# Four slots ahead of the feed-forward, and weights in six slices: a retention layer fused with a bilinear feed-forward

## The chip, the cores and the metric

The kernel runs on one core of a Trainium2 chip. The metric is device microseconds of one execution. Before the change it is 255.87 us, the median of three runs (255.71 to 256.0). The profiled execution, from which all durations below come, has a span of 254.2 us from the first to the last instruction.

## The reference

The first half is a decayed linear attention (retention) over 4 batches, 8 heads, 768 positions and 64 channels a head:

```python
for t in range(S):
    state = gamma * state + outer(k[:, :, t], v[:, :, t])
    y[:, :, t] = scale * q[:, :, t] @ state          # gamma = 1 - 2**(-5 - head)
```

Its output is laid out as x of 3072 tokens by 512 channels and goes through a bilinear feed-forward with d_ff = 1536:

```python
out = ((x @ w_a) * (x @ w_b)) @ w_out
```

Inputs and output are float32.

## The kernel before, in words

**Slots.** A slot is 128 positions of one batch, all heads: 6 slots a batch, 24 in all. For each slot three loads fetch k, q and v (256 KB each, in rows of 256 bytes, `load_slot`, L86). `casts` makes bfloat16 copies: kb (k with its decay, on VectorE for the slots of the first tile, on GpSimd for later ones), qb (GpSimd) and vb (ScalarE for the first tile, else GpSimd). Then three steps run on TensorE. `step_a` transposes kb and qb into PSUM (L181, L183), and VectorE copies both out as kqT (L185). `step_b` forms the scores `at` of the slot from kqT (L193), which VectorE masks into aT (L197), and adds the slot to the running state `st` (L203), which ScalarE copies to gst (L210); the last slot of a batch needs no state. `step_c` forms y from the state (L218, not for the first slot of a batch) and from aT (L223), and ScalarE copies it into xt (L228), where it is the transposed input of the feed-forward.

**Tiles.** `TILES` groups consecutive slots into tiles. For tile J the feed-forward runs 12 blocks (`ffn_ab`): block ft has four matmuls into `a` (L253), which ScalarE copies to asb (L256), and four into `g` (L259), which VectorE multiplies by asb into ht (L261). A matmul is as wide as the tile: 128 columns for each slot. `a` and `g` share three PSUM buffers. Then `ffn_out` runs once for each slot of the tile: 12 matmuls of 512 columns (L266), a copy on ScalarE (L269), and the store (L271).

**Weights.** w_a and w_b are loaded in slices by columns (`load_w`, L93), w_out in four parts by rows (`load_o`, L99), each into a float32 staging tile with a number of buffers (`bufs`), and cast to bfloat16 by `cast_w` and `cast_o` (L143, L145). A slice serves `FPW` blocks: three blocks with four slices. Only tile 0 has to wait for weights; from tile 1 on they are all in place.

**The order.** Each engine runs its instructions strictly in the order of the program, which `seq` fixes. All loads go through SyncE's queue in the order of the list `LOADS`; a load into a staging buffer waits until the cast that reads the buffer's last content is done, and everything behind it in that queue waits too. `run` mixes the blocks of the feed-forward (`work`) with the attention steps of later slots (`todo`): step i is placed just before the work item with number `at[i]`, and the casts of a slot are placed up to `ahead` items before its `step_a`. In the stages of tiles 2 to 6 the steps of the next tile are spread evenly.

**The start.** The first tile's slots run with nothing beside them. Then `ab0` runs the blocks of tile 0, and after the last block of slice j it places the casts of slice j+1. On VectorE that cast (0.95 us) thus stands behind the ht of that block.

Of the kernel before, what the change touches and what calls it, by code (L numbers as in the profile page):

```python
# [9 lines left out]
F32 = mybir.dt.float32  # L10
# [2 lines left out]
ALU = mybir.AluOpType  # L13


TILES = [3, 2, 4, 4, 4, 4, 3]


LOADS = ("s0 s1 s2 w0 w1 s3 w2 s4 w3 o0 o1 o2 o3 "
         + " ".join(f"s{t}" for t in range(5, 24))).split()  # L20


@with_exitstack
def kernel(
# [10 lines left out]
    nc = tc.nc  # L35
    P = 128
# [3 lines left out]
    DM = H * D  # L40
    DFF = moe_w_a.shape[1]
    KT = DM // P
    NFT = DFF // P
    NSLOT = B * NCH
    NW = 4
    WC = DFF // NW
    FPW = NFT // NW
    MID = S // 2

    lg = [math.log(1.0 - 2.0 ** (-5.0 - h)) for h in range(H)]  # L50
# [3 lines left out]
    wstage = ctx.enter_context(tc.tile_pool(name="wstage", bufs=4))  # L54
# [24 lines left out]
    raws, wst = {}, {}  # L79
# [8 lines left out]

    def load_w(j):
        for nm, src in (("a", moe_w_a), ("b", moe_w_b)):  # L90
            st = wstage.tile([P, KT, WC], F32, tag="w" + nm, name="wst" + nm, bufs=2)
            s = src[:, j * WC : (j + 1) * WC].rearrange("(c p) f -> p c f", p=P)
            seq(nc.sync.dma_start(out=st, in_=s))  # L93
            wst[nm, j] = st

    def load_o(j):
        st = wstage.tile([P, FPW, DM], F32, tag="wo", name="wsto", bufs=2)
        s = moe_w_out[j * FPW * P : (j + 1) * FPW * P, :].rearrange("(c p) d -> p c d", p=P)
        seq(nc.sync.dma_start(out=st, in_=s))  # L99
        wst["o", j] = st  # L100

    pending = list(LOADS)

    def issue_loads(n):
        for _ in range(min(n, len(pending))):
            what = pending.pop(0)
            {"s": load_slot, "w": load_w, "o": load_o}[what[0]](int(what[1:]))
# [29 lines left out]
    wa_bf = wpool.tile([P, KT, DFF], BF16, name="wa_bf")  # L137
    wb_bf = wpool.tile([P, KT, DFF], BF16, name="wb_bf")
    wo_bf = wpool.tile([P, NFT, DM], BF16, name="wo_bf")

    def cast(engine, dst, src):
        if engine is nc.scalar:
            seq(nc.scalar.copy(dst, src))  # L143
        else:
            seq(engine.tensor_copy(dst, src))  # L145

    def cast_w(j):
        sl = slice(j * WC, (j + 1) * WC)
        cast(nc.scalar if j == 0 else nc.gpsimd, wa_bf[:, :, sl], wst["a", j])
        cast(nc.vector, wb_bf[:, :, sl], wst["b", j])  # L150

    def cast_o(j):
        cast(nc.gpsimd, wo_bf[:, j * FPW : (j + 1) * FPW, :], wst["o", j])


    kb, qb, vb, kqT, aT = {}, {}, {}, {}, {}
# [2 lines left out]
    first = 0  # L159
    for J, n in enumerate(TILES):  # L160
        for i in range(n):
# [4 lines left out]
    def casts(t):  # L166
        ci = t % NCH
        early = t < TILES[0]
        kb[t] = nat.tile([P, H, D], BF16, tag="kb", name="kb")
        qb[t] = nat.tile([P, H, D], BF16, tag="qb", name="qb")  # L170
        vb[t] = nat.tile([P, H, D], BF16, tag="vb", name="vb")
        seq((nc.vector if early else nc.gpsimd).tensor_tensor(  # L172
            kb[t], raws["k", t], ktab[:, ci, :, :].to_broadcast([P, H, D]), op=ALU.mult))
        seq(nc.gpsimd.tensor_tensor(  # L174
            qb[t], raws["q", t], qtab[:, ci, :, :].to_broadcast([P, H, D]), op=ALU.mult))
        cast(nc.scalar if early else nc.gpsimd, vb[t], raws["v", t])

    def step_a(t):
        tp = psat.tile([P, 2, HP, P], BF16, tag="at", name="tp")
        for hp in range(HP):  # L180
            seq(nc.tensor.transpose(tp[:, 0, hp, :], kb[t][:, 2 * hp : 2 * hp + 2, :], ident))  # L181
        for hp in range(HP):
            seq(nc.tensor.transpose(tp[:, 1, hp, :], qb[t][:, 2 * hp : 2 * hp + 2, :], ident))  # L183
        kqT[t] = tra.tile([P, 2, HP, P], BF16, tag="kqT", name="kqT")
        seq(nc.vector.tensor_copy(kqT[t], tp))  # L185

    def step_b(t):
        ci = t % NCH
        at = [psat.tile([P, HP, P], F32, tag="at", name=f"at{e}") for e in range(2)]
        for hp in range(HP):  # L190
            for e in range(2):
                r = slice(64 * e, 64 * e + 64)
                seq(nc.tensor.matmul(at[e][:, hp, :], kqT[t][r, 0, hp, :], kqT[t][r, 1, hp, :],  # L193
                                     start=True, stop=True))
        aT[t] = tra.tile([P, 2, HP, P], BF16, tag="aT", name="aT")
        for e in range(2):
            seq(nc.vector.tensor_tensor(aT[t][:, e], at[e], mask, op=ALU.mult))  # L197
        if ci < NCH - 1:
            if ci == 0:
                state[0] = psst.tile([P, HP, P], F32, tag="st", name="st")  # L200
            st = state[0]
            for hp in range(HP):
                seq(nc.tensor.matmul(st[:, hp, :], kb[t][:, 2 * hp : 2 * hp + 2, :],  # L203
                                     vb[t][:, 2 * hp : 2 * hp + 2, :],
                                     start=(ci == 0 and hp == 0), stop=(hp == HP - 1),
                                     skip_group_check=True))
            g = gst[(t + 1) % 2]
            for e in range(2):
                r = slice(64 * e, 64 * e + 64)
                seq(nc.scalar.copy(g[r, :, r], st[r, :, r]))  # L210

    def step_c(t):
        ci = t % NCH
        J, i = where[t]
        y = psat.tile([P, HP, P], F32, tag="at", name="y")
        if ci > 0:
            for hp in range(HP):
                seq(nc.tensor.matmul(y[:, hp, :], gst[t % 2][:, hp, :], kqT[t][:, 1, hp, :],  # L218
                                     start=(hp == 0), stop=False, skip_group_check=True))
        for hp in range(HP):  # L220
            for e in range(2):
                r = slice(64 * e, 64 * e + 64)
                seq(nc.tensor.matmul(y[r, hp, :], vb[t][:, 2 * hp + e, :], aT[t][:, e, hp, :],  # L223
                                     start=(ci == 0 and hp == 0), stop=(hp == HP - 1),
                                     skip_group_check=True))
        if i == 0:
            xt[J] = xtp.tile([P, KT, 4 * P], BF16, tag="xt", name="xt")
        seq(nc.scalar.copy(xt[J][:, :, i * P : (i + 1) * P], y))  # L228

    def steps(slots):  # L230

        slots = list(slots)
        todo = []
        for i in range(len(slots) + 1):
            if i < len(slots):
                todo.append((step_a, slots[i]))
            if i > 0:
                todo.append((step_c, slots[i - 1]))
            if i < len(slots):
                todo.append((step_b, slots[i]))  # L240
        return todo
# [4 lines left out]
    def ffn_ab(J, ft):  # L246
        w = TILES[J] * P
        if ft == 0:
# [14 lines left out]
    def ffn_out(J, i):  # L263
# [5 lines left out]
        seq(nc.scalar.copy(osb, o))  # L269
        n0 = (sum(TILES[:J]) + i) * P  # L270
        seq(nc.scalar.dma_start(out=out[n0 : n0 + P, :], in_=osb))  # L271


    def run(work, todo, at, ahead=4):

        order = []
        for g, w in enumerate(work):
            order += [todo[i] for i in range(len(todo)) if at[i] == g]
            order.append(w)
        starts = [s for fn, s in todo if fn is step_a]  # L280
        for i, (fn, *args) in enumerate(order):
            for fn2, *a2 in order[i : i + ahead + 1]:
                if fn2 is step_a and a2[0] in starts:
                    starts.remove(a2[0])
                    casts(a2[0])
            fn(*args)

    def ab0(ft):
        ffn_ab(0, ft)
        if ft % FPW == FPW - 1 and ft // FPW + 1 < NW:  # L290
            cast_w(ft // FPW + 1)

    casts(0)
    casts(1)
    step_a(0)
    casts(2)
    step_b(0)
    step_a(1)
    step_c(0)
    step_b(1)  # L300
    step_a(2)
    step_c(1)
    step_b(2)
    cast_w(0)
    step_c(2)
    issue_loads(100)

    work = [(ab0, ft) for ft in range(NFT)] + [(ffn_ab, 1, ft) for ft in range(6)]
    todo = steps([3, 4])
    run(work, todo, [6, 7, 9, 10, 11, 12], ahead=3)  # L310
    for j in range(NW):
        cast_o(j)
    work = [(ffn_ab, 1, ft) for ft in range(6, NFT)]
    work += [(ffn_out, 0, i) for i in range(TILES[0])]
    work += [(ffn_out, 1, i) for i in range(TILES[1])]
    todo = steps(range(5, 9))
    run(work, todo, [3, 4, 5, 6, 6, 7, 7, 8, 8, 9, 9, 10])
    slot = sum(TILES[:3])
    for J in range(2, len(TILES)):
        n = TILES[J]  # L320
# [2 lines left out]
        todo = steps(nxt)  # L323
        work = [(ffn_ab, J, ft) for ft in range(NFT)] + [(ffn_out, J, i) for i in range(n)]
# [31 lines left out]
```

## Time and profile before

| What | Value |
|---|---|
| median of 3 runs | 255.87 us (255.71 to 256.0) |
| profiled execution, span | 254.2 us |
| TensorE busy | 233.5 us (92%) |
| VectorE, ScalarE, GpSimd busy | 102.2, 91.6, 73.6 us |
| loads through SyncE's queue | 80704 packets, 28.32 MB |
| first feed-forward matmul | 21.54 us |
| first matmul of tile 1 | 47.10 us |
| first matmul of tile 2 | 77.44 us |
| last matmul ends | 250.4 us |

Times within an execution count from the first instruction of the span. PE is TensorE, PEld its weight loads, DVE VectorE, ACT ScalarE, POOL GpSimd and SP SyncE; L253 is line 253 of the kernel. A row of the timeline has the start, the duration, engine, line and operation, output and inputs by the program's names, the shape of one instruction, the number of instructions merged, and in brackets the idle time of the engine before it and what ended that. A row of the waits has who waited for whom, the total in us, how often, and the longest. A busy TensorE is not TensorE at full speed: pitches, the distance from one start to the next, tell the speed. The column for the granted clock reads 1.00 all through this profile, since its first record comes only at 27.0 us; before that the pitch of the matmuls is what shows it.

### The profile page before, as it was taken

How to read it: one execution, taken by the hardware profiler on the slowest of the kernel's cores; microseconds unless marked ns; L12 is line 12 of the kernel's file. 1: busy time of each engine (PE TensorE's matmuls, PEld its weight loads, DVE VectorE, ACT ScalarE, POOL GpSimd, SP SyncE). 2: the span in 40 equal slices, each digit the busy share in tenths (PEclk: the TensorE clock that was granted, in tenths of full speed). 3: DMA queues.
4: the chain of work that ended last, by engine and by line, in shares of the span. 5: the costliest groups of instructions: out<-in, count | busy, mean ns of one | idle time of the engine just before them, and what ended most of it. 6: DMA issues, size and time to landing. Idle time of an engine off the chain costs nothing.

```text
span 254.2 us, 4303 instructions
## 1 busy us (share of the span) xinstructions
PE 233.5 (92%) x1672; PEld 127.0 (50%) x1696; DVE 102.2 (40%) x173; ACT 91.6 (36%) x179; POOL 73.6 (29%) x84
## 2 busy tenths in 40 slices
PE   0487889899999999999999999999999999999994
PEld 0363445786555455445455445445445454446641
DVE  1462375465325456305455306455205465104410
ACT  2154233534243442423434412444314333223311
POOL 5115474286757667503133403000000000000000
PEclk9999999999999999999999999999999999999999
DMA  7999997999999999969910021000021000120012
GB/s 155 219 358 289 303 292 257 296 217 205 252 239 271 209 214 220 191 173 274 183 32 3 3 112 55 0 0 3 24 100 44 0 0 3 41 97 27 3 41 84
DMA packets 84181, 34.88 MB, mean 137 GB/s; under 512 B 75457, under 2 KB 79553, under 8 KB 84161
## 3 DMA queue, kind: packets, MB, share of 16 engines
q1 hardware_dynamic: 80704, 28.32, 50.1%
q10 hardware_dynamic: 3456, 6.29, 6.7%
q8 instruction: 13, 0.21, 0.4%
q14 instruction: 8, 0.06, 0.1%
HBM read 28.31 MB, written 6.29 MB: 136 GB/s over the span
## 4 chain that ended last, share of the span: by engine, by line
PE 88%; SPq 3%; DMA 2%; ACT 2%; DVE 2%; issue 2%; DVEq 0%; ACTq 0%
PE g L259 25%; PE a L253 25%; PE o L266 24%; PE y L223 3%; PE at L193 3%; SPq L86 3%; PE st L203 3%; DMA vf<-in_v_dram 2%; PE tp L181 2%; PE tp L183 2%; PE y L218 2%; DVE wb_bf L145 1%; ACT gst L210 1%; ACT wa_bf L143 1%; ACT xt L228 0%
## 5 line engine op out<-in xcount | busy, mean ns | idle before, releaser
L261 DVE TENSOR_TENSOR ht<-g,asb 128x512 bf16<-128x512 f32 (+2 forms) x84 | 51.6, 615 | 86.8 <-PE g L259 69.2
L253 PE MATMUL a<-xt,wa_bf 128*128 128x512 bf16 (+2 forms) x325 | 76.6, 354 | 2.7 <-ACT xt L228 2.3
L259 PE MATMUL g<-xt,wb_bf 128*128 128x512 bf16 (+2 forms) x332 | 76.5, 353 | 2.6 <-DVE wb_bf L145 2.5
L256 ACT CAST asb<-a 128x512 bf16<-128x512 f32 (+2 forms) x84 | 44.0, 524 | 70.6 <-PE a L253 56.1
L266 PE MATMUL o<-wo_bf,ht 128*128 128x512 bf16 x279 | 63.5, 379 | 0.6 <-issue 0.2
L259 PEld LDWEIGHTS <-wb_bf 128*128 128x128 bf16 x336 | 33.0, 99 | 33.5 <-DVE wb_bf L145 3.6
L266 PEld LDWEIGHTS <-ht 128*128 128x128 bf16 x288 | 27.4, 98 | 31.6
L253 PEld LDWEIGHTS <-wa_bf 128*128 128x128 bf16 x336 | 30.7, 99 | 24.6 <-issue 2.7
L197 DVE TENSOR_TENSOR aT<-at,mask 128x512 bf16<-128x512 f32 x48 | 30.7, 681 | 7.0 <-PE at L193 7.0
L172 POOL TENSOR_TENSOR kb<-kf,ktab 128x512 bf16<-128x512 f32 x21 | 21.9, 1042 | 37.0 <-DMA kf<-in_k_dram 16.7
L185 DVE COPY kqT<-tp 128x1024 bf16<-128x1024 bf16 x24 | 16.4, 683 | 38.4 <-PE tp L183 38.4
L269 ACT COPY osb<-o 128x512 f32<-128x512 f32 x24 | 14.0, 585 | 46.7 <-PE o L266 36.7
L174 POOL TENSOR_TENSOR qb<-qf,qtab 128x512 bf16<-128x512 f32 x24 | 25.0, 1042 | 11.7 <-DMA qf<-in_q_dram 11.2
L210 ACT CAST gst<-st 64x256 bf16<-64x256 f32 x40 | 14.6, 366 | 15.5 <-PE st L203 15.1
L228 ACT CAST xt<-y 128x512 bf16<-128x512 f32 x24 | 14.0, 585 | 15.9 <-PE y L223 13.4
L145 POOL CAST vb<-vf 128x512 bf16<-128x512 f32 x21 | 13.5, 644 | 20.9 <-issue 14.9
L181 PE MATMUL tp<-ident,kb 128*128 128x128 bf16 x96 | 10.0, 230 | 5.0 <-DVE kb L172 5.0
L223 PE MATMUL y<-aT,vb 128*64 128x128 bf16 x192 | 11.1, 235 | 2.1 <-DVE aT L197 2.1
L193 PE MATMUL at<-kqT 64*128 64x128 bf16 x192 | 10.2, 230 | 2.5 <-DVE kqT L185 2.0
L181 PEld LDWEIGHTS <-kb 128*128 128x128 bf16 x96 | 7.7, 103 | 9.1 <-DVE kb L172 5.0
L193 PEld LDWEIGHTS <-kqT 64*128 64x128 bf16 x192 | 5.8, 98 | 10.5 <-issue 7.1
L183 PE MATMUL tp<-ident,qb 128*128 128x128 bf16 x96 | 10.0, 231 | 0.9 <-POOL qb L174 0.9
(28 smaller groups left out, 68.0 us busy)
## 6 DMA issues: line engine op xcount, KB each, us to landing
kf<-in_k_dram SPq DMA_DIRECT2D x24, 256.0 KB, 5.1
qf<-in_q_dram SPq DMA_DIRECT2D x24, 256.0 KB, 5.1
vf<-in_v_dram SPq DMA_DIRECT2D x24, 256.0 KB, 5.1
out_dram<-osb ACTq DMA_DIRECT2D x24, 256.0 KB, 2.1
wsta<-in_moe_w_a_dram SPq DMA_DIRECT2D x4, 768.0 KB, 6.5
wstb<-in_moe_w_b_dram SPq DMA_DIRECT2D x4, 768.0 KB, 7.6
wsto<-in_moe_w_out_dram SPq DMA_DIRECT2D x4, 768.0 KB, 7.3
```

The costliest lines, as they stand in the source:

```text
L172: seq((nc.vector if early else nc.gpsimd).tensor_tensor(kb[t], raws["k", t], ktab[:, ci, :, :].to_broadcast([P, H, D]), op=ALU.mult))
L174: seq(nc.gpsimd.tensor_tensor(qb[t], raws["q", t], qtab[:, ci, :, :].to_broadcast([P, H, D]), op=ALU.mult))
L181: seq(nc.tensor.transpose(tp[:, 0, hp, :], kb[t][:, 2 * hp : 2 * hp + 2, :], ident))
L193: seq(nc.tensor.matmul(at[e][:, hp, :], kqT[t][r, 0, hp, :], kqT[t][r, 1, hp, :], start=True, stop=True))
L197: seq(nc.vector.tensor_tensor(aT[t][:, e], at[e], mask, op=ALU.mult))
L210: seq(nc.scalar.copy(g[r, :, r], st[r, :, r]))
L223: seq(nc.tensor.matmul(y[r, hp, :], vb[t][:, 2 * hp + e, :], aT[t][:, e, hp, :], start=(ci == 0 and hp == 0), stop=(hp == HP - 1), skip_gr ...
L253: seq(nc.tensor.matmul(a, wa_bf[:, kt, fs], xt[J][:, kt, :w], start=(kt == 0), stop=(kt == KT - 1)))
L256: seq(nc.scalar.copy(asb, a))
L259: seq(nc.tensor.matmul(g, wb_bf[:, kt, fs], xt[J][:, kt, :w], start=(kt == 0), stop=(kt == KT - 1)))
L261: seq(nc.vector.tensor_tensor(ht[J][:, ft, :w], g, asb, op=ALU.mult))
L266: seq(nc.tensor.matmul(o, ht[J][:, ft, i * P : (i + 1) * P], wo_bf[:, ft, :], start=(ft == 0), stop=(ft == NFT - 1)))
```

## The change

The first tile has four slots and the last one two: (4, 2, 4, 4, 4, 4, 2). All four slots of tile 0 go through attention before the first block, in another order of casts and steps. w_a and w_b come in six slices of 256 columns (512 KB, rows of 1 KB) with three staging buffers each instead of two; w_out keeps four parts. In the load queue slot 3 moves ahead of the weights, slot 5 ahead of slice 3. ScalarE casts all slices of w_a (before: the first; GpSimd the others). The casts of slice j+1 follow the first block of slice j instead of its last. The steps of slots 4 and 5 are placed within tile 0; those of slots 6 to 9 all lie among the output blocks of tiles 0 and 1.

```diff
-TILES = [3, 2, 4, 4, 4, 4, 3]
+TILES = [4, 2, 4, 4, 4, 4, 2]
-LOADS = ("s0 s1 s2 w0 w1 s3 w2 s4 w3 o0 o1 o2 o3 "
-         + " ".join(f"s{t}" for t in range(5, 24))).split()
+LOADS = ("s0 s1 s2 s3 w0 w1 s4 w2 s5 w3 w4 w5 o0 o1 o2 o3 "
+         + " ".join(f"s{t}" for t in range(6, 24))).split()
...
-    NW = 4
+    NW = 6
     WC = DFF // NW
     FPW = NFT // NW
+    NO = 4
+    FPO = NFT // NO
...
-            st = wstage.tile([P, KT, WC], F32, tag="w" + nm, name="wst" + nm, bufs=2)
+            st = wstage.tile([P, KT, WC], F32, tag="w" + nm, name="wst" + nm, bufs=3)
...
-        cast(nc.scalar if j == 0 else nc.gpsimd, wa_bf[:, :, sl], wst["a", j])
+        cast(nc.scalar, wa_bf[:, :, sl], wst["a", j])
         cast(nc.vector, wb_bf[:, :, sl], wst["b", j])
...
-        if ft % FPW == FPW - 1 and ft // FPW + 1 < NW:
+        if ft % FPW == 0 and ft // FPW + 1 < NW:
             cast_w(ft // FPW + 1)
 
     casts(0)
+    step_a(0)
     casts(1)
-    step_a(0)
-    casts(2)
     step_b(0)
     step_a(1)
+    casts(2)
     step_c(0)
     step_b(1)
     step_a(2)
+    casts(3)
     step_c(1)
     step_b(2)
+    step_a(3)
+    step_c(2)
+    step_b(3)
     cast_w(0)
-    step_c(2)
+    step_c(3)
     issue_loads(100)
 
-    work = [(ab0, ft) for ft in range(NFT)] + [(ffn_ab, 1, ft) for ft in range(6)]
-    todo = steps([3, 4])
-    run(work, todo, [6, 7, 9, 10, 11, 12], ahead=3)
-    for j in range(NW):
+    work = [(ab0, ft) for ft in range(NFT)]
+    run(work, steps([4, 5]), [5, 6, 8, 9, 10, 11], ahead=4)
+    for j in range(NO):
         cast_o(j)
-    work = [(ffn_ab, 1, ft) for ft in range(6, NFT)]
+    work = [(ffn_ab, 1, ft) for ft in range(NFT)]
     work += [(ffn_out, 0, i) for i in range(TILES[0])]
     work += [(ffn_out, 1, i) for i in range(TILES[1])]
-    todo = steps(range(5, 9))
-    run(work, todo, [3, 4, 5, 6, 6, 7, 7, 8, 8, 9, 9, 10])
+    todo = steps(range(6, 10))
+    run(work, todo, [12, 13, 13, 14, 14, 14, 15, 15, 16, 16, 17, 17])
```

`load_o` and `cast_o` use `FPO` where they used `FPW`, which is three blocks as before. `steps` lists a of the first slot, b of it, a of the second, c of the first, b of the second, and so on.

More of the change, by code (lines that the diff above doesn't have):

```diff
@@ L96, in load_o @@
     def load_o(j):
-        st = wstage.tile([P, FPW, DM], F32, tag="wo", name="wsto", bufs=2)
-        s = moe_w_out[j * FPW * P : (j + 1) * FPW * P, :].rearrange("(c p) d -> p c d", p=P)
+        st = wstage.tile([P, FPO, DM], F32, tag="wo", name="wsto", bufs=2)
+        s = moe_w_out[j * FPO * P : (j + 1) * FPO * P, :].rearrange("(c p) d -> p c d", p=P)
         seq(nc.sync.dma_start(out=st, in_=s))
@@ L148, in cast_w @@
         sl = slice(j * WC, (j + 1) * WC)
-        cast(nc.scalar if j == 0 else nc.gpsimd, wa_bf[:, :, sl], wst["a", j])
+        cast(nc.scalar, wa_bf[:, :, sl], wst["a", j])
         cast(nc.vector, wb_bf[:, :, sl], wst["b", j])
     def cast_o(j):
-        cast(nc.gpsimd, wo_bf[:, j * FPW : (j + 1) * FPW, :], wst["o", j])
+        cast(nc.gpsimd, wo_bf[:, j * FPO : (j + 1) * FPO, :], wst["o", j])
     kb, qb, vb, kqT, aT = {}, {}, {}, {}, {}
```

## The prediction

> **What bounds the kernel now.** I read the page from the top: busy shares, the chain that ended last, then TensorE's waits, then the first 90 us instruction by instruction, then the DMA stream alone. The page:
>
> ```profile
> PE 233.5 (92%) x1672; PEld 127.0 (50%) x1696; DVE 102.2 (40%) x173; ACT 91.6 (36%) x179; POOL 73.6 (29%) x84
> ...
> PE 88%; SPq 3%; DMA 2%; ACT 2%; DVE 2%; issue 2%; DVEq 0%; ACTq 0%
> ```
>
> TensorE is the bound, and the matmul work is fixed: in both tile lists the widths sum to 24 slots over 7 tiles, and the pitch of one matmul is 0.109, 0.1625 and 0.2157 us at 256, 384 and 512 columns, so 4+2 or 3+3 slots cost the same. Only idle time and half-speed time can move. TensorE's waits:
>
> ```profile
> PE tp L181 <- DVE kb L172: 5.0, 1, 5.0
> PE g L259 <- DVE wb_bf L145: 2.5, 3, 1.1
> PE a L253 <- ACT xt L228: 2.3, 2, 1.6
> ```
>
> The timeline of the first 40 us shows where they lie, and the clock:
>
> ```profile
> 21.54 1.44 PE L253 MATMUL a<-xt,wa_bf 128*128 128x384 bf16 x4 [1.58 <-ACT xt L228]
> ...
> 24.65 1.04 POOL L174 TENSOR_TENSOR qb<-qf,qtab 128x512 bf16<-128x512 f32 x1
> ...
> 26.94 0.61 POOL L145 CAST vb<-vf 128x512 bf16<-128x512 f32 x1 [1.25 <-DMA vf<-in_v_dram]
> ...
> 28.85 0.95 DVE L145 CAST wb_bf<-wstb 128x1536 bf16<-128x1536 f32 x1
> ...
> 29.85 0.82 PE L259 MATMUL g<-xt,wb_bf 128*128 128x384 bf16 x4 [0.94 <-DVE wb_bf L145]
> 30.51 0.81 PE L253 MATMUL a<-xt,wa_bf 128*128 128x384 bf16 x4
> ...
> 35.29 0.68 DVE L185 COPY kqT<-tp 128x1024 bf16<-128x1024 bf16 x1
> ```
>
> The first feed-forward matmul starts at 21.54. Four matmuls take 1.28 us (start to start) until 26.6 and 0.65 after: TensorE runs at half speed for about 5.4 us of the tile, a loss of 2.7. Then g waits for a `wb_bf` cast three times: counted against the 0.65 pitch, 1.10 at 29.85, 1.22 at 35.43 and 0.66 at 41.10, in all 2.98; and the first matmul of tile 1 waits 0.75 for `xt` at 47.10. From 76.99 (first transpose of slot 9) the pitch is unbroken to 250.3.
>
> The DMA stream alone, in three stretches with one packet size each (7 to 12 us: 256-byte rows of q, k, v; 14 to 21: 1536-byte rows of the weights; 39 to 41.5: 2048-byte rows of w_out):
>
> ```profile
> DMA packets 4356, 1.10 MB, mean 220 GB/s; under 512 B 4356, under 2 KB 4356, under 8 KB 4356
> ...
> DMA packets 1768, 2.64 MB, mean 377 GB/s; under 512 B 48, under 2 KB 1768, under 8 KB 1768
> ...
> DMA packets 501, 0.99 MB, mean 397 GB/s; under 512 B 16, under 2 KB 16, under 8 KB 501
> ```
>
> The queue is full from 4 us to 31 us, so landings follow each other at these rates: by the completion events of the trace v of slot 2 lands at 13.67, then four 768 KB slices at 15.79, 17.90, 20.03, 22.23 (2.12 each), then k and q of slot 3 at 23.41 and 24.58 (1.18 each).
>
> **The change part by part.**
>
> *Four slots before the feed-forward.* Three more loads put v3 at 13.67 + 3 x 1.18 = 17.2, q3 at 16.05. From there the durations of before: qb3 on POOL 16.15 to 17.2 (1.04), transposes 0.61, kqT 17.9 to 18.6 (0.68), at 0.61, aT 19.5 to 20.75 (1.28), y to 21.4. kb3 moves from POOL to DVE (0.69) and vb3 to ScalarE (0.62), both inside load waits. ScalarE meanwhile does xt2, gst3 (to 20.8), the first cast of wa (1.47 x 1024/1536 = 0.98, to 21.8) and xt3 to 22.4. The feed-forward starts at 22.45 instead of 21.54, with one slot more behind it. The half-speed time stays: if the clock rises again at 27.0, 4.5 us, a loss of 2.3.
>
> *Casts one f-block earlier and wa on ScalarE.* cast_w follows the first block of a slice, not its last: the cast (DVE 0.95 x 2/3 = 0.63 to 0.65; ACT 0.98) has a whole block of 1.725 us (8 x 0.2157) to hide in, so the 2.98 go where data has landed. c of slot 5 stands one block ahead of tile 1, so the 0.75 goes.
>
> *Six slices: when they land.* A 512 KB slice is 512 packets of 1 KB. One packet costs 256/220 = 1.16 ns, 1536/377 = 4.07 ns, 2048/397 = 5.16 ns of the stream; on the line between the first two 1 KB costs 2.91 ns, on the line through the last two 2.98: 1.49 to 1.53 us a slice. Ends: 1.40 (the rate of the 1.5 KB rows) and 2.12 (a 1 KB packet as dear as a 1.5 KB one). I take 1.52, from the two nearest rows. In the new order w3's b lands after slots 3, 4, 5 (9 x 1.18 = 10.6) and 8 slices (12.2): 13.7 + 22.8 = 36.5. On top comes one lag: at 23.42 a 16 KB packet of the instruction queue held one DMA engine 1.28 us, v3 landed 2.31 instead of 1.18 after q3 (the vb row at 26.94), and first-to-last spread stayed near 1.7 us (0.5 before) until the stream paused at 31. It came at TensorE's 200th instruction, which the new order reaches before its feed-forward, so I add 1.2: L = 37.7 (ends: none, 36.5; two such packets, 38.9). The third staging buffer lifts the pause: before, SyncE held w3's a until POOL had cast w1's a (31.0).
>
> *The new wait.* DVE runs in program order: wb slice 3 is now queued after ht of block 4 and ahead of kqT of slot 4, ht of block 5 and aT of slot 4. TensorE is ready for slot 4's at-matmuls at 22.45 + 6 x 1.725 + 2.27 + 0.45 = 35.5, but kqT comes at L + 0.08 + 0.65 + 0.68 and at-matmuls at L + 1.50 = 39.2 (one cast took 1.51 beside POOL at 33.86; POOL has nothing to do at L; end +0.4): TensorE stands still for 3.7 us. The start, the half-speed time and the earlier casts lie in that cover: up to 3.7 us of them is free. Later slices (40.7, 43.8) are wanted on DVE at 42.4 and 46.4, so they hold nothing; w_out moves behind two more slices and a slot: its first part lands near 46, and the last two, each waiting for a staging buffer as before (landings 6.2 and 9.4 after the first there: 41.27, 47.46, 50.70), are cast by about 58; it is wanted at 63. q of slot 9 lands near 69 and is wanted by 76. Both are hidden by 5 us or more, POOL's part too.
>
> *From L to the end.* Block pitch 1.725; a attention step costs 0.45 (a), 0.57 to 0.67 (b), 0.67 (c, 0.35 without state), read from the starts of the rows. Slot 4's b to the end of tile 0: 0.57 + 6 x 1.725 + 0.45 + 0.67 + 0.43 + 0.67 = 13.1. Tile 1: 24 x 0.4367 = 10.5. Then six output blocks (72 x 0.2157 = 15.5) with slots 6 to 9, 6.6 by the starts of 60 to 77, plus one new wait: c of slot 9 directly follows its b, so y waits for aT: at 0.40, aT 1.28, two hand-overs 0.12, less 0.89 of issued matmuls, 0.9 (ends 0 and 1.6, the longest y wait before). Sum 23.1. Slot 10 starts at L + 1.5 + 13.1 + 10.5 + 23.1 = L + 48.2 = 85.9, against slot 9 at 76.99. From there the stages of before took 37.75, 38.20, 37.75, 36.20 and 23.36; with 14 attention slots instead of 15 and a last tile of 2 they come to 37.75, 37.95, 37.9, 34.4 and 15.65 = 163.65, 9.6 less. With the 4.0 after TensorE's end: L + 215.85 = 253.55, against 254.23: 0.7 less. The profiled execution's 254.2 lies 1.6 below the median 255.87, so I forecast 255.2.
>
> *Rules weighed.* The trace first: an idle start ran 5.4 us at half speed, and after that no idle stretch is over 1.2 us. The Trainium skill, "TensorE: Matmul & The Clock Gate", section "Why this matters for your kernels", warns of idle gaps over about 3 us, after which the clock halves again; it speaks against this change with its 3.7. By its window of 3.4 us, one or two of them at half speed, the sum would be 1.7 to 3.4 longer, 256.9 to 258.6, an estimate from that page. No row of before has such a gap.
>
> The slices of before land 2.12 us apart. The skill's "DMA: Bandwidth & Descriptors", section "Anatomy of one DMA", gives about 2.0 us fixed plus bytes at 436 GB/s, 3.8 for a 768 KB slice and 3.2 for 512 KB: by it, as an estimate, eight slices would land 13 us later. The row decides: in a full queue the fixed part is hidden.
>
> **The rivals.**
>
> *Dearer slices (slower).* Everything after 39 us hangs on L, with 8 slices in it. From 1.61 us a slice the gain is gone; at 2.12 it is 4.1 slower. For it: packets of 256 bytes run at 220 GB/s, so small ones are dear. Against: 1.5 to 2 KB changes the rate by 5%. Middle of it, 1.75: 257.
>
> *The gap costs the clock.* After 3.7 idle the half speed returns for as long as at first (5.4 us, a loss of 2.7): 258. For it: the half speed of the start. Against: no row shows that a pause after full speed does it.
>
> *No lag.* The instruction packet falls before the weights or its engine catches up: L = 36.5, 254.0. At the 1.40 slice as well 253.0, the lowest sum I can make.
>
> *The change does not do what it says.* The casts of wb slices 4 and 5 hold g as before, 0.66 to 1.22 each: 1.3 to 2.4 more, 256.5 to 257.6. Against: two blocks last 3.45 on TensorE, and DVE's most in two blocks (two ht 0.69, a cast 0.65, a kqT 0.68) is 2.7.
>
> **How the numbers follow.** This kernel's runs differ by 0.1%; 0.2% (0.5 us) is what a measurement can tell from no change. Chances: the forecast 0.55 (own range 254.6 to 255.9), no lag 0.15, dearer slices 0.14, the clock 0.08, casts that still hold g 0.08. Of the forecast 0.34 lies under 255.36 and 0.17 between that and 256.38. Faster by over 0.2%: 0.34 + 0.15 = 0.49. Same: 0.17 and 0.02 of dearer slices, 0.19. Slower: the rest, 0.32. Range: 253.6, between no lag and its own lower end, to 257.5, past the middle of dearer slices; outside lie its worst and the clock.
>
> **What would show it.** Right: first feed-forward matmul near 22.4; no g wait for wb_bf; one at wait (L195 in the new file) of 3 to 4 us ending near 39; y of slot 9 waiting 0.9; slot 10 near 86. Wrong: w slices landing over 1.6 apart, pitch doubled after 39, or wb slice 4 or 5 waited for as well.

## The result and the profile after

The changed kernel takes 257.97 us (median of 5 runs, 257.17 to 259.12), the kernel before 256.0 in the same comparison (255.71 to 256.6): ratio 1.0075, with a 95% interval of 1.0055 to 1.0094. It is slower by 0.75%, where 255.2 was forecast and 257.5 was the upper end of the range.

The profiled execution of the changed kernel has a span of 256.5 us. Its lines have moved by two (the at-matmuls are L195, g is L261, the cast of wb L147). TensorE's waits:

```profile
PE at L195 <- DVE kqT L187: 4.9, 3, 3.9
PE tp L183 <- DVE kb L174: 4.9, 1, 4.9
...
PE a L255 <- ACT wa_bf L145: 0.8, 1, 0.8
PE y L225 <- DVE aT L199: 0.8, 3, 0.4
...
PE g L261 <- DVE wb_bf L147: 0.2, 1, 0.2
```

The waits of g for its cast, 2.5 before, are down to 0.2, and the first matmul of tile 1 no longer waits. In their place stands one wait of 3.9 us, that of slot 4's at-matmuls for kqT. VectorE's timeline of the changed kernel says why:

```profile
37.71 0.69 DVE L147 CAST wb_bf<-wstb 128x1024 bf16<-128x1024 f32 x1 [3.96 <-DMA wstb<-in_moe_w_b_dram]
38.32 0.68 DVE L187 COPY kqT<-tp 128x1024 bf16<-128x1024 bf16 x1
```

The cast of wb slice 3 waits for its landing at 37.69, and kqT stands behind it. TensorE's timeline across that place, still of the changed kernel:

```profile
33.23 1.03 PE L255 MATMUL a<-xt,wa_bf 128*128 128x512 bf16 x4
34.09 1.03 PE L261 MATMUL g<-xt,wb_bf 128*128 128x512 bf16 x4
39.06 0.61 PE L195 MATMUL at<-kqT 64*128 64x128 bf16 x8 [3.94 <-DVE kqT L187]
39.60 0.61 PE L205 MATMUL st<-vb,kb 128*128 128x128 bf16 x4
40.00 1.91 PE L255 MATMUL a<-xt,wa_bf 128*128 128x512 bf16 x4
41.71 1.91 PE L261 MATMUL g<-xt,wb_bf 128*128 128x512 bf16 x4
43.41 1.73 PE L255 MATMUL a<-xt,wa_bf 128*128 128x512 bf16 x4
44.98 1.03 PE L261 MATMUL g<-xt,wb_bf 128*128 128x512 bf16 x4
```

Ahead of the pause four matmuls of 512 columns have a pitch of 0.86 us; after it 1.71, twice as long, until 44.8. The same in the table of stretches (the last three columns are granted clock, DMA share and GB/s):

```profile
22.83:35.12 12.29, 11.31 (x56) 4.88 (x55) 4.66 (x7) 4.82 (x7) 5.23 (x6) 1.00 1.11 248
35.12:39.06 3.94, 0.00 (x1) 0.01 (x2) 1.35 (x3) 1.53 (x2) 0.22 (x1) 0.87 1.10 349
39.06:45.84 6.78, 6.78 (x28) 2.96 (x29) 3.12 (x5) 2.85 (x5) 0.07 (x1) 0.57 1.07 364
45.84:54.98 9.14, 9.14 (x74) 4.68 (x72) 5.16 (x8) 4.37 (x7) 4.69 (x3) 1.00 0.73 225
```

By the clock records of this trace the clock fell to one half at 38.00, inside the pause, and rose at 44.83. Work went on at 39.06, so 5.77 us ran at half speed: 2.9 lost. Everything else came as summed: slot 10 starts at 88.68, which is the forecast's 85.9 and 2.8 more, and the rest of the span is 167.8, as forecast.

### The profile page after: what moved, and what is told of

It is laid out like the page before. It is cut to its first block, busy times and chain, and to the rows that moved or that the text cites. A ratio compares the mean times of both kernels' runs of the same rounds, so it can differ in the third digit from the quotient of the medians.

```text
span 256.5 us, 4335 instructions
## 1 busy us (share of the span) xinstructions
PE 236.8 (92%) x1696; PEld 127.6 (50%) x1696; DVE 103.1 (40%) x176; ACT 96.2 (38%) x185; POOL 66.7 (26%) x79
## 4 chain that ended last, share of the span: by engine, by line
PE 83%; SPq 9%; DMA 4%; ACT 1%; issue 1%; DVE 1%; ACTq 0%; DVEq 0%
PE o L268 25%; PE a L255 24%; PE g L261 22%; SPq L88 8%; PE at L195 3%; PE y L225 3%; DMA wstb<-in_moe_w_b_dram 2%; PE st L205 2%; DMA wsta<-in_moe_w_a_dram 2%; PE tp L183 2%; PE tp L185 2%; PE y L220 1%; SPq L95 1%; ACT osb L271 0%; ACT wa_bf L145 0%
## 5 line engine op out<-in xcount | busy, mean ns | idle before, releaser
L263 DVE TENSOR_TENSOR ht<-g,asb 128x512 bf16<-128x512 f32 (+1 forms) x84 | 51.7, 615 | 83.3 <-PE g L261 71.5
L255 PE MATMUL a<-xt,wa_bf 128*128 128x512 bf16 (+1 forms) x336 | 77.7, 355 | 2.2 <-ACT xt L230 1.4
L261 PE MATMUL g<-xt,wb_bf 128*128 128x512 bf16 (+1 forms) x336 | 76.9, 352 | 0.4 <-ACT asb L258 0.2
L258 ACT CAST asb<-a 128x512 bf16<-128x512 f32 (+1 forms) x84 | 44.0, 525 | 63.4 <-PE a L255 61.9
L268 PE MATMUL o<-wo_bf,ht 128*128 128x512 bf16 x288 | 64.5, 379 | 0.0
L261 PEld LDWEIGHTS <-wb_bf 128*128 128x128 bf16 x336 | 33.1, 99 | 31.0 <-issue 1.7
L271 ACT COPY osb<-o 128x512 f32<-128x512 f32 x24 | 14.1, 586 | 49.4 <-PE o L268 39.4
L174 POOL TENSOR_TENSOR kb<-kf,ktab 128x512 bf16<-128x512 f32 x20 | 21.0, 1049 | 38.1 <-PE st L205 18.2
L147 POOL CAST vb<-vf 128x512 bf16<-128x512 f32 x20 | 12.2, 610 | 20.6 <-issue 16.8
L195 PE MATMUL at<-kqT 64*128 64x128 bf16 x192 | 10.6, 237 | 4.9 <-DVE kqT L187 4.9
L195 PEld LDWEIGHTS <-kqT 64*128 64x128 bf16 x192 | 6.0, 101 | 13.7 <-issue 7.2
## 6 DMA issues: line engine op xcount, KB each, us to landing
kf<-in_k_dram SPq DMA_DIRECT2D x24, 256.0 KB, 5.2
qf<-in_q_dram SPq DMA_DIRECT2D x24, 256.0 KB, 5.1
vf<-in_v_dram SPq DMA_DIRECT2D x24, 256.0 KB, 5.1
out_dram<-osb ACTq DMA_DIRECT2D x24, 256.0 KB, 2.1
```

Source lines behind the costliest of these rows:

```text
L174: seq((nc.vector if early else nc.gpsimd).tensor_tensor(kb[t], raws["k", t], ktab[:, ci, :, :].to_broadcast([P, H, D]), op=ALU.mult))
L255: seq(nc.tensor.matmul(a, wa_bf[:, kt, fs], xt[J][:, kt, :w], start=(kt == 0), stop=(kt == KT - 1)))
L258: seq(nc.scalar.copy(asb, a))
L261: seq(nc.tensor.matmul(g, wb_bf[:, kt, fs], xt[J][:, kt, :w], start=(kt == 0), stop=(kt == KT - 1)))
L263: seq(nc.vector.tensor_tensor(ht[J][:, ft, :w], g, asb, op=ALU.mult))
L268: seq(nc.tensor.matmul(o, ht[J][:, ft, i * P : (i + 1) * P], wo_bf[:, ft, :], start=(ft == 0), stop=(ft == NFT - 1)))
```

## The experiments

**Theory.** The pause of 3.9 us brought the clock down; the 2 to 3 us lost at half speed after it make the kernel slower instead of a little faster. The cause of the pause is the place of slot 5 in the load list. **Rivals:** the fall of the clock is chance or hidden elsewhere, and the wait alone counts; or the new place of the casts is what the change lives on.

**The pause filled.** Twelve matmuls that nobody reads, behind block 5:

```diff
     def ab0(ft):
         ffn_ab(0, ft)
+        if ft == 5:
+            fill = psff.tile([P, 4 * P], F32, tag="ff", name="fill")
+            for i in range(12):
+                seq(nc.tensor.matmul(fill, wa_bf[:, i % KT, :P], xt[0][:, i % KT, :],
+                                     start=(i == 0), stop=(i == 11)))
```

> The changed kernel, with twelve more matmuls of 512 columns (12 x 0.2157 = 2.6 us) put into TensorE's pause between block 5 and the at-matmuls of slot 4; nothing reads them. The pause (35.1 to 39.1, ended by wb slice 3 and kqT) stays where the loads set it. Clock theory: the pause alone made the clock fall at 38.0, and half speed from 39.1 to 44.8 cost 2.9 us; with the pause filled the clock holds, and the span is 256.5 - 2.9 = 253.6 although TensorE does more work (median near 255.1). Rival (the fall of the clock is chance, or its time would be hidden elsewhere): span 256.5, median near 258.

Measured: span 253.5 in the profile, 253.5 to 254.6 in ten runs, mean clock 0.998 to 1.000 in all of them; median 256.15 (255.57 to 256.68), ratio to before 0.9992 (0.9975 to 1.0009). TensorE's timeline of this kernel:

```profile
36.17 2.75 PE L295 MATMUL fill<-xt,wa_bf 128*128 128x512 bf16 x12
38.86 0.40 PE L195 MATMUL at<-kqT 64*128 64x128 bf16 x8
39.19 0.40 PE L205 MATMUL st<-vb,kb 128*128 128x128 bf16 x4
39.42 1.03 PE L255 MATMUL a<-xt,wa_bf 128*128 128x512 bf16 x4
40.29 1.03 PE L261 MATMUL g<-xt,wb_bf 128*128 128x512 bf16 x4
```

The at-matmuls start where they did (38.86 against 39.06) but what follows has its full pitch of 0.86. From there to the end of the span it takes 214.7 us against 217.4 in the changed kernel, 2.8 less; 2.9 is what the clock records gave. (In this profile the first blocks ran at half speed until 28.3, so TensorE came to the pause 1.1 us later and the twelve matmuls fill it wholly.) More work on the busiest engine made the kernel 1.8 us faster at the median. The first rival falls: the clock's fall is on the path, and the pause makes it. What is left without the fall is as fast as the kernel before, not 0.7 us faster: the median span is 0.3 shorter than that of the kernel before in this comparison (254.1 against 254.4), and the time outside the span is some 0.35 longer.

**Half filled.** The same with five matmuls:

> The changed kernel with five instead of twelve matmuls in the pause (1.1 us): TensorE is idle for 2.8 us instead of 3.9. If a pause must last a whole window of 3.4 us to bring the clock down, every run stays at full speed: span 253.6, as with twelve. If a window that is mostly idle is enough, some runs lose one window at half speed: spans from 253.6 up to 255.3, and a mean clock of 0.992 to 0.993 in the longer ones.

Measured: 256.77 (255.48 to 258.1), ratio 1.0011 (0.9984 to 1.0039). The eight runs fall into two kinds: four with a mean clock of 0.991 to 0.993 and spans of 255.1 to 256.1, four with 0.997 to 1.000 and 253.4 to 254.4. The profiled one is of the first kind (TensorE's busy time is the first after the length, the clock third from the right):

```profile
30.00:36.00 6.00, 5.95 (x33) 2.71 (x32) 2.12 (x4) 1.72 (x3) 2.67 (x3) 1.00 1.18 268
36.00:39.11 3.11, 0.35 (x9) 0.20 (x8) 1.55 (x3) 1.53 (x2) 0.00 (x0) 1.00 1.09 350
39.11:42.52 3.41, 3.41 (x19) 1.49 (x14) 1.59 (x3) 1.59 (x4) 0.00 (x0) 0.50 1.10 349
42.52:46.00 3.48, 3.48 (x23) 1.81 (x22) 2.46 (x4) 1.26 (x2) 0.36 (x1) 1.00 1.05 385
```

The profile shows a pause of 2.76 us and after it one stretch of 3.41 us at half speed. For the other runs there is only the mean clock, which doesn't say where the time was lost: one such stretch makes 0.993 of this span. That their spans fall into the same two kinds, 255.2 and 253.9 at the medians, speaks for the pause, since half-speed time ahead of it would lie in its cover. As far as this tells, a pause of 2.8 us costs one window in four of eight runs, and none in the others.

**kqT ahead of the cast.** One position in the list of steps:

```diff
-    run(work, steps([4, 5]), [5, 6, 8, 9, 10, 11], ahead=4)
+    run(work, steps([4, 5]), [4, 6, 8, 9, 10, 11], ahead=4)
```

> The changed kernel with the transposes of slot 4 one block earlier, so that kqT stands on VectorE ahead of the cast of wb slice 3. The at-matmuls then run at once; block 6 waits for wa slice 3 (lands 36.2, cast by 37.25), and its g for wb slice 3 until 38.4, which is 2.1 us less than the way through kqT; the pause comes in two pieces of under 2 us. Clock theory: the clock holds: 256.5 - 2.1 - 2.9 = 251.5 span, median near 253. Rival (only the wait counts): 254.4 span, median near 256.

Measured: 254.71 (253.51 to 256.01), ratio 0.993 (0.9901 to 0.9958); the profiled span is 253.3. TensorE's timeline of this kernel:

```profile
37.44 1.56 PE L255 MATMUL a<-xt,wa_bf 128*128 128x512 bf16 x4 [2.11 <-ACT wa_bf L145]
38.80 1.91 PE L261 MATMUL g<-xt,wb_bf 128*128 128x512 bf16 x4
40.50 1.39 PE L255 MATMUL a<-xt,wa_bf 128*128 128x512 bf16 x4
41.73 1.03 PE L261 MATMUL g<-xt,wb_bf 128*128 128x512 bf16 x4
```

The wait is 2.1 instead of 3.9, and here even that brought the clock down, from 37.8 to 41.2. In three of ten runs the mean clock is 0.992 to 0.993 (spans 253.3 to 254.0), in seven 0.997 or more (251.4 to 252.8). I had expected that pieces of about 2 us hold the clock, and in three runs this one did not. The two kinds lie near 251.5, the clock theory's span, and near 253.2, the same with one window lost (1.7). The rival's 254.4 leaves the clock out altogether; that it comes near the slower kind means nothing.

**Slot 5 behind slice 3.** One edit in the load list:

```diff
-LOADS = ("s0 s1 s2 s3 w0 w1 s4 w2 s5 w3 w4 w5 o0 o1 o2 o3 "
+LOADS = ("s0 s1 s2 s3 w0 w1 s4 w2 w3 s5 w4 w5 o0 o1 o2 o3 "
```

> The changed kernel with one edit in the load list: slot 5 after slice 3 instead of before it. wb slice 3 lands 3 x 1.18 = 3.5 us earlier, near 34.1, and the at-matmuls wait for well under 1 us; slot 5 and slices 4 and 5 come when they are wanted. Clock theory: no pause, no fall: tile 1 starts 5.5 us earlier (49.4 instead of 55.0), span near 251.0, median near 252.6, below the kernel before. Rival (the clock falls anyhow near there): 253.9 span, 255.5 median.

Measured: 253.13 (252.95 to 253.16), ratio 0.9869 (0.9838 to 0.99), span 251.1. VectorE's timeline of this kernel at the same place:

```profile
33.96 0.69 DVE L147 CAST wb_bf<-wstb 128x1024 bf16<-128x1024 f32 x1 [0.31 <-DMA wstb<-in_moe_w_b_dram]
34.57 0.68 DVE L187 COPY kqT<-tp 128x1024 bf16<-128x1024 bf16 x1
```

and TensorE's:

```profile
35.31 0.40 PE L195 MATMUL at<-kqT 64*128 64x128 bf16 x8 [0.29 <-DVE kqT L187]
...
35.88 1.03 PE L255 MATMUL a<-xt,wa_bf 128*128 128x512 bf16 x4
```

The slice lands 3.75 us earlier (33.94 instead of 37.69), the wait is 0.29, the clock holds, tile 1 starts at 49.58 (forecast for this run 49.4; 54.98 in the changed kernel). Slot 5's three loads, 3.5 us of the stream, had stood ahead of a slice whose cast here starts at 33.96, 5.4 us before the first transposes of slot 5 (39.33). One edit turns 0.75% slower into 1.3% faster than before, and the runs spread by 0.2 us instead of 2.

**The casts late again.** One part undone:

```diff
-        if ft % FPW == 0 and ft // FPW + 1 < NW:
+        if ft % FPW == FPW - 1 and ft // FPW + 1 < NW:
```

> The changed kernel with one part undone: the casts of slice j+1 stand again behind the last block of slice j, not its first. kqT of slot 4 is then ahead of the cast of wb slice 3; TensorE pauses less than 2 us at block 6 (for wa slice 3, until 37.3, and wb slice 3, until 38.5), but g of blocks 2, 8 and 10 waits 0.8 us each for its cast. Tile 1 starts near 52.0 instead of 55.0. Clock theory: the clock holds, or falls for one window: span 253.5 to 255.2. Rival (the earlier cast is what the change gains, the clock is a side matter): 5 x 0.8 = 4 us slower than the changed kernel, 260.

Measured: 256.25 (255.29 to 257.22), ratio 0.9995 (0.9972 to 1.0019), spans 253.2 to 255.2, clock 0.997 or more in all ten runs. Undoing this part of the change makes it 1.7 us faster, since kqT then stands ahead of the slice's cast and the longest pause is 1.9 us. The blocks wait about as long as expected, though for ScalarE's cast of wa more than for VectorE's of wb: 4.2 in five waits against 0.7 in one. The second rival falls.

**Four slices.** The kernel with slot 5 behind slice 3, with slices of 768 KB:

```diff
-LOADS = ("s0 s1 s2 s3 w0 w1 s4 w2 w3 s5 w4 w5 o0 o1 o2 o3 "
+LOADS = ("s0 s1 s2 s3 w0 w1 s4 w2 w3 s5 o0 o1 o2 o3 "
...
-    NW = 6
+    NW = 4
```

> The kernel with slot 5 after slice 3 (span 251.1), with four slices of 768 KB instead of six of 512 KB (three staging buffers, casts behind the first of three blocks); load order s0 s1 s2 s3 w0 w1 s4 w2 w3 s5. wb slice 2 now lands near 35 and its cast (0.95) stands ahead of ht of block 4 and kqT of slot 4: the at-matmuls come near 37.5 instead of 35.3, after two pauses of 1.2 and 1.7 us. If smaller slices are worth something here: 2.2 us longer, span 253.3, and up to 1.7 more where the clock falls for one window. Rival (the slices don't matter, only their order does): 251.1.

Measured: 255.93 (255.66 to 256.75), ratio 0.9973 (0.9949 to 0.9996), span 254.4. TensorE's timeline of this kernel:

```profile
37.52 0.40 PE L195 MATMUL at<-kqT 64*128 64x128 bf16 x8 [0.56 <-DVE kqT L187]
...
42.59 0.40 PE L183 MATMUL tp<-ident,kb 128*128 128x128 bf16 x4 [0.89 <-POOL kb L174]
43.59 0.40 PE L185 MATMUL tp<-ident,qb 128*128 128x128 bf16 x4 [0.60 <-POOL qb L176]
```

The at-matmuls come at 37.52, where I had put them: wb slice 2 landed at 35.28. In this profile the first blocks ran at half speed to 29.0, but that lay in the cover of this landing, for which VectorE waited 1.45 us. What I had not seen is that slot 5, now behind all four large slices, is late as well, by 1.5 us. At the medians four slices are 2.8 us slower than six in this load order. About half of that, by this profile, is slot 5's place, and whether another order would suit four slices better was not tried.

**Three staging buffers alone,** in the kernel before:

```diff
-            st = wstage.tile([P, KT, WC], F32, tag="w" + nm, name="wst" + nm, bufs=2)
+            st = wstage.tile([P, KT, WC], F32, tag="w" + nm, name="wst" + nm, bufs=3)
```

> The kernel before, with three staging buffers instead of two and nothing else. SyncE's queue then no longer stands still at 31 us for the cast of wa slice 1, and wb slice 3 lands up to 2 us earlier than 39.05. If the loads set the kernel before, the span falls by up to 1 us (g of block 9 waits 0.66 for that slice). If the place of the cast behind ht sets its waits, as its trace shows: no change, 254.2.

Measured: 256.24 (255.79 to 257.0), ratio 0.9984 (0.9962 to 1.0005). The third buffer alone changes nothing, and the loads didn't move as expected: SyncE issues wa slice 3 at 31.03 (30.98 before), and wb slice 3 lands at 38.86 instead of 39.05. So it was not the staging buffer that held the queue there.

That the loads don't hold the kernel before doesn't follow. In this profile the clock rose at 19.47 instead of 26.99, so the first blocks ran at full speed, and yet the span is 254.6. Its timeline shows where the gain went:

```profile
36.81 1.47 POOL L145 CAST wa_bf<-wsta 128x1536 bf16<-128x1536 f32 x1 [1.67 <-DMA wsta<-in_moe_w_a_dram]
38.33 0.82 PE L253 MATMUL a<-xt,wa_bf 128*128 128x384 bf16 x4 [1.54 <-POOL wa_bf L145]
38.88 0.96 DVE L145 CAST wb_bf<-wstb 128x1536 bf16<-128x1536 f32 x1 [1.87 <-DMA wstb<-in_moe_w_b_dram]
...
39.90 1.45 PE L259 MATMUL g<-xt,wb_bf 128*128 128x384 bf16 x4 [0.75 <-DVE wb_bf L145]
```

Both casts of slice 3 wait for their loads, and TensorE for both casts. These two waits, 1.54 and 0.75 us, also brought the clock down, from 39.95 to 43.36 by its records, although neither is as long as 2 us. So in this execution the loads do hold the kernel there. Since the third buffer changed nothing, the kernel before should do the same when its clock rises early, but no profile with two buffers shows it.

**A long pause in the kernel before.** Five operations on VectorE ahead of its cast of slice 3 (`scrf` and `scro` are 128 x 512 scratch tiles, float32 and bfloat16):

```diff
     def cast_w(j):
+        if j == 3:
+            for _ in range(5):
+                seq(nc.vector.tensor_tensor(scro, scrf, scrf, op=ALU.mult))
```

> The kernel before, with five more operations of 0.69 us on VectorE (3.45 us) ahead of its cast of wb slice 3, whose result nobody reads: g of block 9 then waits from 40.4 to 44.6, 4.1 us instead of 0.66. Clock theory: one stretch at half speed of one or two windows of 3.4 us follows: 254.2 + 3.45 + 1.7 to 3.4 = 259.4 to 261.1 span. Rival (a pause costs its own length): 257.7 span.

One execution: 263.06, span 261.3. One of the five took 1.83 us, so the pause came out longer than I had planned. Stretches of this kernel:

```profile
40.39:46.50 6.11, 0.00 (x1) 0.00 (x1) 6.01 (x6) 0.48 (x1) 3.03 (x2) 0.74 0.64 211
46.50:50.18 3.68, 3.68 (x21) 1.96 (x22) 1.10 (x2) 0.59 (x1) 1.47 (x1) 0.50 0.98 328
```

TensorE idles for 6.11 us and then runs for 3.68 at half speed (1.84 lost). The pause's own length over the 0.5 by which the page's count has it before is 5.6: 259.8 by the rival, 261.6 with the clock, 261.3 measured. From the end of the pause to the end of the span it takes 214.8 us, against 213.1 before (from 41.10): 1.7 more. In this one execution the kernel before loses its clock in the same way.

**One wait less.** In the kernel with slot 5 behind slice 3, the steps of slots 6 to 9 are spread otherwise, so that c of slot 9 doesn't directly follow its b:

```diff
-    run(work, todo, [12, 13, 13, 14, 14, 14, 15, 15, 16, 16, 17, 17])
+    run(work, todo, [12, 13, 13, 14, 14, 14, 15, 15, 15, 16, 16, 17])
```

> The kernel with slot 5 after slice 3 (span 251.1), with one more edit: the last steps of slots 6 to 9 are placed so that b of slot 9 comes one output block earlier and c of slot 9 no longer follows it directly. If y of slot 9 waited for its aT alone, the 0.85 us that its row is longer than the others goes and nothing comes back: span 250.3, median 252.3. Rival (the wait moves to the transposes of slot 9, whose q is the last to land): 251.1, no change.

Measured: 252.06 (251.67 to 252.33), ratio 0.9834 (0.9813 to 0.9856), span 249.9. The waits of y for aT go from 0.8 to 0.2 us, and none comes in their place. Slot 10 starts 1.15 us earlier (82.13 against 83.28); 0.65 of that arises after the start of tile 1, where the edit is, and the other 0.5 ahead of it, which is not the edit's. This is the fastest version: 4.2 us under the kernel before at the medians of this comparison (252.06 against 256.26), 1.7% by the ratio.

## Why the prediction was wrong, point by point

- **The step that failed is the clock after the pause.** The sum paid the pause by its length alone and put the clock after it at nothing; the runs show 1.8 us at the medians and 2.9 in the profile. I had the pause, its place, its cause and nearly its length (3.7; measured 3.94), and the rival "the gap costs the clock" described what came. The prediction even names the sign, a pitch doubled after 39. But I gave that rival 0.08 and let the range end below it, because no row of before had such a gap. A missing row is no evidence against. What I did have were the half speed of the start and the warning in the Trainium skill, "TensorE: Matmul & The Clock Gate", section "Why this matters for your kernels", both on the rival's side. That the rival's 258 equals the measured 257.97 is partly luck: its clock cost was 2.7, the medians show 1.8, and two other terms make up the rest.
- **What the clock cost.** In the profiled execution 2.9 us; over runs, medians of the spans, 255.9 against 254.1 with the pause filled: 1.8. Three of the changed kernel's five runs have a mean clock of 0.991 or 0.992 (spans 255.1 to 255.9), two 0.986 or 0.987 (256.5, 257.1): one or two windows.
- **The rest of the miss.** 257.97 less 255.2 is 2.77: 1.8 from the clock; 0.55 since the filled kernel's median span is 254.1 and not 253.55; and 0.4 outside the span, which the sum took from before (1.6 to 1.7) and which is 2.06 here.
- **Right: the landings.** wb slice 3 landed at 37.69, forecast 37.7, and with it the place of the wait (39.06; 39.2). Slices of 512 KB landed 1.50 apart; I took 1.52, so dearer slices fall as a rival. The fixed part of about 2.0 us a load that the prediction weighed and set aside is given in its source for loads that GpSimd issues, while these go through SyncE; landings 1.50 apart show nothing of it. The lag came too: a 16 KB instruction packet at 21.61 held one engine 1.16 us, and the slice that landed at 24.70 came 2.30 after the one before. That is 0.8 where I had put 1.2, and it came at TensorE's 248th instruction, not at the 200th; the first slice landed 1.96 after v of slot 3, 0.5 more than the 1.50. That the whole comes out within 0.1 is in part luck.
- **Right, without effect: the start.** The first feed-forward matmul came at 22.83 (22.45) and at full speed, since the clock had risen at 20.93; I had put 2.3 us of half speed there. All that lay in the pause's cover, as said. TensorE was ready at 35.12 (35.5) by errors that nearly cancel: 2.3 less for the half speed, 0.4 more for the later start, and 1.5 more for waits and slower rows at slice 2, which I had at nothing.
- **Right: g's waits went** (2.5 to 0.2) and that of tile 1; new small ones of 0.8 and 0.2 for slice 2 also lay in the cover. y of slot 9 waited, 0.85 in the row's length and 0.65 by removing it (0.9 forecast). From slot 10 on 167.8 us, as summed.
- **Read wrongly, without effect on the sum.** The staging buffer did not make the queue pause at 31 us, as the kernel before with three buffers shows. The spread of 0.1% was that of three runs; in the later comparisons the kernel before runs from 255.3 to 258.3. The last terms up to slot 10 add up to 23.0, not 23.1 (measured 23.1).

## What to carry to other kernels

A wait on TensorE is not paid by its length alone: where the sum makes a pause of 2 us or more, add the half speed after it, 1.7 us of lost work for one window and up to 2.9 in these runs. Waits that follow each other closely count together: 1.54 and 0.75 us were enough. Where loads are the limit, order the list by when each is wanted, and look at what stands behind a cast that waits for a load on an engine that runs in order: here 3.5 us of loads that nobody wanted yet cost 4.8 us at the median (257.97 against 253.13), more than the change gains with the order mended. If a pause can't be removed, matmuls in it that nobody reads are cheaper than the half speed after it.

## What the runs showed of the hardware that I had not expected

- The clock changes only at edges 3.41 us apart: up at 20.93, down at 38.00, up at 44.83 in the changed kernel (5 and 2 such steps), and 19.46, 22.88, 26.29, 43.36, 50.18 in the kernel with the long pause. This agrees with the free-running window in the Trainium skill, "TensorE: Matmul & The Clock Gate", section "What's actually happening". The limit of about 3 us for a gap in its section "Why this matters for your kernels" is too generous here: single pauses of 2.18 us were enough in three of ten runs and 2.76 in four of eight (by mean clock and span), and so were 1.54 and 0.75 together. In these traces it is the idle time between two edges that tells. Six times the clock fell after a window in which TensorE was idle for 1.95 to 2.96 of the 3.41 us, so it needn't be idle throughout; the longest that it outlived is 1.74. The wait of 1.9 in the kernel with the late casts, which held in ten of ten runs, is cut by an edge in its profile, with 1.65 on one side.
- The clock's first rise varies between executions from 16.8 to 29.0 us, in kernels with nearly the same start. An early rise needn't shorten the span: at 19.47 and 26.99 the kernel before, with three buffers and with two, took 254.6 and 254.2. How much of its spread from 255.3 to 258.3 is the clock's isn't shown.
- The time outside the span is 2.0 to 2.1 us with six slices (in the changed kernel and those with its slices) and 1.6 to 1.8 with four, also where only the slices and their loads differ. Why is open.
